# Operand and x transposes moved to DMA, and the hash to 32x32 VectorE transposes with row and column tiles, in a hash-bucketed attention kernel with a gated feed-forward part

## The chip, the cores and the metric

One core of one Trainium2 chip. The metric is the device time of one execution in microseconds (us), lower is better. Executions of one kernel were repeated; medians of them are given. A run is called slow when it is more than 1.5% above the fastest of the same kernel, else fast. A median over slow and fast runs is not comparable between kernels, so differences below are taken between the means of fast runs.

## The reference, cut to what matters

```python
def _attn_ref(q, k, v, proj):                 # q, k, v: (4, 8, 768, 64) float32; proj: (64, 6)
    q_bits = (einsum('bhsd,dk->bhsk', q, proj) > 0)      # 6 hash bits per token
    k_bits = (einsum('bhsd,dk->bhsk', k, proj) > 0)
    mask = q_bucket[:, :, :, None] == k_bucket[:, :, None, :]   # buckets from the bits
    scores = where(mask, q @ k^T / 8, -1e9)
    return softmax(scores) @ v
x = attn_out.transpose(0, 2, 1, 3).reshape(3072, 512)
def _moe_ref(x, w_gate, w_val, w_out, w_res): # 512 -> 1536 -> 512
    ffn_out = (gelu(x @ w_gate) * (x @ w_val)) @ w_out
    return x + sigmoid(x @ w_res) * ffn_out
```

The mask costs no instruction of its own. Each operand of a score matmul has 64 feature rows, 6 rows of bits (+-0.5) and one constant row, 71 in all. With q scaled by 1/C, C = 2048, a pair of different buckets loses at least half a unit in the score (one bit that differs turns +0.25 into -0.25), and the exponential, which multiplies by C/8 = 256, makes it zero.

## The kernel before

16 pairs of heads, two pairs to a group, so eight groups. A group is prepared in one piece while the group ahead of it runs: loads, fp32 transposes of q and k on TensorE, evacuation by VectorE, casts, hash, bit copies.

```python
def prep(g):
    for pi in range(2):                                   # two pairs
        for side, src in ((0, q), (1, k)):
            nc.sync.dma_start(s, ...)                     # 384 KB
            for (c0, n) in CH:                            # TensorE transposes, fp32 128x128
                for c in range(n):
                    nc.tensor.transpose(ps[:, bass.ts(c, P)], s[:, hi, bass.ts(tp, P)], ident)
                nc.vector.tensor_scalar_mul(tt[...], ps[...], (1.0 / C) if side == 0 else 1.0)
            nc.gpsimd.tensor_copy(ag[0:D, :, 0, :], t3[0:D])
            nc.vector.tensor_copy(ag[0:D, :, 1, :], t3[D:2 * D])
        ...                                               # v: load, casts, sum (unchanged)
    for (t0, n) in CH:                                    # hash: 128 rows, 32 columns per tile
        for pi in range(2):
            for side in range(2):
                nc.tensor.matmul(hs[32 * j:32 * j + 32, :n * P], projw, t32[pi, side][...], ...)
        nc.vector.tensor_scalar(bits[...], hs[...], 0.0, cst, op0=ALU.is_gt, op1=ALU.add)
    ...                                                   # 8 bit copies by DMA into aug[D:KA]

def attn(p):
    for c in range(0, len(bk), 2):                        # 9 steps per pair, 18 per group
        sp = sc_ps.tile([P, 1024], FP32, tag="sp")
        ...  nc.tensor.matmul(sp[...], ks[...], qs[...])  # scores: 71 rows, 1024 columns in all
        nc.scalar.activation(e, sp, AF.Exp, scale=float(ALPHA))
        ...  nc.tensor.matmul(av[hi][:, qt, :], e[...], va[...])   # 8 value products, 65 columns
```

Ahead of the value products of each head stands one more matmul, 128x128 on 390 columns, which starts their sum ("av<-vsum,eps_sb" in the timelines): four of these initial products to a group.

After attention comes a dense feed-forward part whose matmuls are all 128 x 128 x 512.

The softmax here doesn't subtract the row's maximum and nothing guards it: scores larger than these inputs give would overflow.

## Time and profile before

| kernel before | value | where from |
|---|---|---|
| median time | 421.25 us (418.3 to 421.97) | 3 runs |
| first score matmul | 30.9 us | timeline |
| attention, first score to last exponential's use | 31 to 209 us | sums over stretches |
| exponentials | 144, 1.02 us each | group lines |
| feed-forward | 211.7 us | timeline |
| TensorE busy in attention | 157.3 of 178 us | sums over stretches |

The lines behind these are in the prediction. Two more matter later, because the prediction did not look at them. They are TensorE groups kept apart by shape, kernel before; the columns are count, busy us, mean ns of one, idle time before them.

```profile
L212 PE MATMUL sp<-aug,aug 71*128 71x512 bf16 x192 | 66.2, 388 | 0.0
L137 PE MATMUL tp<-ident,ld 128*128 128x128 f32 x192 | 33.9, 314 | 7.6 <-DMA ld<-in_q_dram 3.9 <-DVE t L139 3.6
```

A score matmul of 512 columns takes 388 ns in the mean, in a kernel whose work between the scores includes 192 transposes that use the whole 128 x 128 array. "71\*128" is the part of the array that a matmul uses: 71 rows, 128 columns.

### The profile page before, as it was taken

How to read it: one execution, taken by the hardware profiler on the slowest of the kernel's cores; microseconds unless marked ns; L12 is line 12 of the kernel's file. 1: busy time of each engine (PE TensorE's matmuls, PEld its weight loads, DVE VectorE, ACT ScalarE, POOL GpSimd, SP SyncE). 2: the span in 40 equal slices, each digit the busy share in tenths (PEclk: the TensorE clock that was granted, in tenths of full speed). 3: DMA queues.
4: the chain of work that ended last, by engine and by line, in shares of the span. 5: the costliest groups of instructions: out<-in, count | busy, mean ns of one | idle time of the engine just before them, and what ended most of it. 6: DMA issues, size and time to landing. Idle time of an engine off the chain costs nothing.

```text
span 421.1 us, 7282 instructions
## 1 busy us (share of the span) xinstructions
PE 381.9 (91%) x2924; PEld 199.4 (47%) x2944; DVE 184.3 (44%) x315; ACT 200.2 (48%) x242; POOL 101.2 (24%) x157
## 2 busy tenths in 40 slices
PE   1788988879989898989799999999999999999995
PEld 1454555645565456545444444444444444444442
DVE  1674362936355274631234433344343334334433
ACT  1008879587977768789643123223213313312321
POOL 4961662835558362720000000000000000000000
PEclk9999999999999699999899999999999999999999
DMA  7802728348184732300000110010020010011001
GB/s 244 279 8 86 263 83 297 104 141 298 37 296 158 239 141 86 112 10 2 2 0 0 51 51 2 25 75 2 5 81 15 0 76 25 0 52 50 1 27 75
DMA packets 23138, 36.82 MB, mean 87 GB/s; under 512 B 4672, under 2 KB 16960, under 8 KB 23104
## 3 DMA queue, kind: packets, MB, share of 16 engines
q1 hardware_dynamic: 23104, 36.35, 24.9%
q8 instruction: 23, 0.38, 0.4%
q14 instruction: 11, 0.09, 0.1%
HBM read 29.36 MB, written 6.29 MB: 85 GB/s over the span
## 4 chain that ended last, share of the span: by engine, by line
PE 67%; ACT 10%; DVE 8%; DMA 5%; issue 4%; POOL 3%; SPq 2%; ACTq 0%; DVEq 0%; POOLq 0%
PE gps L276 15%; PE vps L282 15%; PE fps L294 15%; ACT e L217 10%; PE sp L212 6%; PE av L230 5%; PE rps L288 5%; DVE t L139 3%; DVE aug L145 3%; PE tp L137 3%; DMA wtmp<-in_moe_w_out_dram 2%; PE hs L166 2%; DMA ld<-in_k_dram 2%; DMA ld<-in_q_dram 1%; SPq L176 1%
## 5 line engine op out<-in xcount | busy, mean ns | idle before, releaser
L217 ACT ACTIVATE e<-sp 128x1024 bf16<-128x1024 f32 x144 | 140.4, 1021 | 63.6 <-PE sp L212 59.4
L212 PE MATMUL sp<-aug,aug 71*128 71x256 bf16 (+1 forms) x384 | 86.9, 332 | 0.0
L279 ACT ACTIVATE gt<-gps 128x512 bf16<-128x512 f32 x72 | 43.0, 597 | 88.5 <-PE gps L276 85.1
L284 DVE TENSOR_TENSOR hh<-gt,vps 128x512 bf16<-128x512 bf16 x72 | 49.5, 687 | 74.0 <-PE vps L282 67.0
L230 PE MATMUL av<-va,e 128*128 128x65 bf16 x1152 | 61.7, 196 | 14.5 <-ACT e L217 10.5
L276 PE MATMUL gps<-x_sb,wg 128*128 128x512 bf16 x282 | 73.9, 383 | 0.3
L282 PE MATMUL vps<-x_sb,wv 128*128 128x512 bf16 x283 | 73.2, 379 | 0.3
L230 PEld LDWEIGHTS <-e 128*128 128x128 bf16 x1152 | 46.3, 99 | 53.7 <-ACT e L217 49.0
L294 PE MATMUL fps<-wo,hh 128*128 128x512 bf16 x281 | 65.5, 379 | 0.4
L139 DVE TENSOR_SCALAR t<-tp 128x512 f32<-128x512 f32 x64 | 32.8, 550 | 28.1 <-PE tp L137 24.8
L276 PEld LDWEIGHTS <-wg 128*128 128x128 bf16 x288 | 28.4, 99 | 34.6 <-issue 1.1
L144 POOL CAST aug<-t 64x768 bf16<-64x768 f32 x32 | 33.9, 1063 | 45.1 <-DVE t L139 24.9
L282 PEld LDWEIGHTS <-wv 128*128 128x128 bf16 x288 | 28.2, 98 | 34.3 <-issue 0.5
L294 PEld LDWEIGHTS <-hh 128*128 128x128 bf16 x288 | 28.2, 98 | 34.0
L291 ACT ACTIVATE th<-rps 128x512 f32<-128x512 f32 x24 | 14.3, 597 | 61.7 <-PE rps L288 58.9
L137 PE MATMUL tp<-ident,ld 128*128 128x128 f32 x192 | 33.9, 314 | 7.6 <-DMA ld<-in_q_dram 3.9
L298 DVE SCALAR_TENSOR_TENSOR o<-th,fps 128x512 f32<-128x512 f32 x24 | 16.5, 687 | 52.4 <-PE fps L294 49.6
L212 PEld LDWEIGHTS <-aug 71*128 71x128 bf16 x384 | 29.3, 99 | 8.4 <-issue 1.0
L137 PEld LDWEIGHTS tp<-ident,ld 128*128 128x128 f32 x192 | 25.7, 161 | 14.0 <-DVE t L139 6.8
L201 DVE RECIPROCAL rec<-av 128x6 f32<-128x6 f32 x32 | 6.1, 192 | 54.9 <-PE av L230 54.9
L145 DVE CAST aug<-t 64x768 bf16<-64x768 f32 x32 | 28.9, 904 | 2.6 <-PE sp L212 1.7
L288 PE MATMUL rps<-wr,x_sb 128*128 128x512 bf16 x94 | 25.1, 387 | 0.3 <-issue 0.2
(34 smaller groups left out, 186.9 us busy)
## 6 DMA issues: line engine op xcount, KB each, us to landing
ld<-in_q_dram SPq DMA_DIRECT2D x16, 384.0 KB
ld<-in_k_dram SPq DMA_DIRECT2D x16, 384.0 KB
ldv<-in_v_dram SPq DMA_DIRECT2D x16, 384.0 KB
out_dram<-o SPq DMA_DIRECT2D x24, 256.0 KB
wtmp<-in_moe_w_gate_dram SPq DMA_DIRECT2D x4, 768.0 KB
wtmp<-in_moe_w_val_dram SPq DMA_DIRECT2D x4, 768.0 KB
wtmp<-in_moe_w_out_dram SPq DMA_DIRECT2D x4, 768.0 KB
aug<-bits SPq DMA_DIRECT2D x64, 10.5 KB
```

Source lines behind the costliest of these rows:

```text
L137: nc.tensor.transpose(ps[:, bass.ts(c, P)], s[:, hi, bass.ts(tp, P)], ident)
L139: nc.vector.tensor_scalar_mul(tt[:, c0 * P:(c0 + n) * P], ps[:, :n * P], (1.0 / C) if side == 0 else 1.0)
L145: nc.vector.tensor_copy(ag[0:D, :, 1, :], t3[D:2 * D])
L212: nc.tensor.matmul(sp[:, off:off + nq * P], ks[hi][:, bass.ts(jt, P)], qs[hi][:, qt0 * P:(qt0 + nq) * P], start=True, stop=True)
L217: nc.scalar.activation(e, sp, AF.Exp, scale=float(ALPHA))
L230: nc.tensor.matmul(av[hi][:, qt, :], e[:, off:off + P], va[:, hi, jt, 0:D + 1], start=False, stop=(jt == T - 1), skip_group_check=True)
L276: nc.tensor.matmul(gps, wg[:, kk, bass.ts(m, P)], xr[:, kk, :], start=(kk == 0), stop=(kk == KM - 1))
L279: nc.scalar.activation(gt, gps, AF.Gelu)
L282: nc.tensor.matmul(vps, wv[:, kk, bass.ts(m, P)], xr[:, kk, :], start=(kk == 0), stop=(kk == KM - 1))
L284: nc.vector.tensor_mul(hh[:, m, :], gt, vps)
L288: nc.tensor.matmul(rps, xr[:, kk, bass.ts(tt, P)], wr[:, kk, :], start=(kk == 0), stop=(kk == KM - 1))
L294: nc.tensor.matmul(fps, hh[:, m, bass.ts(tt, P)], wo[:, m, :], start=(m == 0), stop=(m == KF - 1))
```

## The change

Its intent is to take the transposes off TensorE and to let prep run in small pieces between the scores. Operands are cast to bf16 (zero padded from 64 to 128 columns) and transposed by DMA; x is transposed by DMA too; the hash takes 32x32 block transposes of the fp32 data from VectorE, and multiplies them in 32-row, 32-column tiles of the array, several at once; the conversion, hash and weight loads are handed out one piece per exponential; the value products lag one exponential behind. Cut to its core:

```diff
-                        for c in range(n):
-                            nc.tensor.transpose(ps[:, bass.ts(c, P)], s[:, hi, bass.ts(tp, P)], ident)
-                        nc.vector.tensor_scalar_mul(tt[...], ps[:, :n * P], ...)
+                n = nat[(2 * p + side) % NN]              # 128 x 12 x 128 bf16, half of it zeros
+                nc.gpsimd.tensor_copy(n[:, :, 0:D], s)
+                nc.sync.dma_start_transpose(out=ag, in_=n.rearrange("p c n -> p (c n)"))
+                nc.vector.transpose(tt..., s...)          # 32x32 blocks, fp32
...
-                        nc.tensor.matmul(hs[32 * j:32 * j + 32, :n * P], projw, t32[pi, side][...])
+            for a0 in (0, 2):
+                for c0, c1 in ((0, HT // 2), (HT // 2, HT)):
+                    for dh in range(2):
+                        for j, t in enumerate(src):       # four operands: column tile j
+                            for i in range(2):            # row tile a = a0 + i
+                                nc.tensor.matmul(hs[i][32 * j:32 * j + 32, c0:c1, :],
+                                    projw[32 * a:32 * a + 32, dh, :],
+                                    t[32 * a:32 * a + 32, c0:c1, dh, :],
+                                    start=(dh == 0), stop=(dh == 1),
+                                    tile_position=(32 * a, 32 * j))
+                    yield                                 # one piece of side work
...
         def xpose(b):
-            for kk in range(KM):  ... nc.tensor.transpose(...); nc.vector.tensor_copy(...)
+            for t in range(b * T, (b + 1) * T):
+                nc.sync.dma_start_transpose(out=x_sb[:, t], in_=x_tok[:, t, :])
...
+        def ahead(g):                                     # side work of group g, in pieces
+            convert(2g+2); yield; convert(2g+3); yield
+            load(2g+4); load(2g+5); three weight pieces (g >= 1); yield
+            yield from hashes((2g+2, 2g+3))               # ends with 4 bit copies by DMA
```

The score and value matmuls are unchanged in shape and number.

## The prediction

> **What bounds the kernel now.** I read the page first (engine shares, the 40 slices, the groups), then the sums over three stretches, then the timeline of a quiet piece and of the start, and last the chain in order of time where it stalls. The first group line gives the exponentials of the attention, the sums over stretches give the stages.

> ```profile
> span 421.1 us, 7282 instructions
> L217 ACT ACTIVATE e<-sp 128x1024 bf16<-128x1024 f32 x144 | 140.4, 1021 | 63.6 <-PE sp L212 59.4
> 0.00:31.00 31.00, 17.89 (x83) 10.77 (x84) 16.40 (x30) 1.28 (x1) 21.88 (x48) 1.00 0.55 180
> 31.00:208.00 177.00, 156.50 (x1903) 94.58 (x1902) 84.75 (x166) 140.36 (x144) 79.35 (x109) 0.98 0.41 140
> 208.00:421.10 213.10, 207.54 (x940) 94.07 (x958) 83.11 (x121) 58.59 (x97) 0.00 (x0) 0.99 0.08 30
> ```

> There are three stages. Up to 31 us nothing is exponentiated. From 31 to 208 us 144 exponentials run, 140.4 of 177 us. From 208 us on the feed-forward part keeps TensorE busy for 207.5 of 213.1 us. The change leaves that last stage's 960 matmuls as they are (only the strides of x differ), so what can be won lies in the first 208 us. A quiet piece shows the pace that attention could have:

> ```profile
> 185.80 5.08 ACT L217 ACTIVATE e<-sp 128x1024 bf16<-128x1024 f32 x5
> 187.79 0.42 PE L230 MATMUL av<-va,e 128*128 128x65 bf16 x8
> 188.05 0.60 PE L212 MATMUL sp<-aug,aug 71*128 71x256 bf16 x3
> 188.91 0.42 PE L230 MATMUL av<-va,e 128*128 128x65 bf16 x8 [0.26 <-ACT e L217]
> ```

> Five exponentials in 5.08 us are 1.016 us each. TensorE needs 188.05-187.79 = 0.26 us for eight value products and about 0.44 us for 1024 score columns (1024 in two such calls of 0.60 us, less a tail of about 0.17), so 0.70 us per exponential: 0.32 us of it is slack. A group of two pairs is 18 exponentials, 18.3 us at this pace; eight groups are 146 us. The stage takes 177, so 31 us are lost there, to prep work that holds TensorE's queue and to two DMA stalls, which the chain shows:

> ```profile
> 114.76 5.95 DMA ld<-in_q_dram
> 120.71 1.20 POOL aug L144
> 121.91 1.42 POOL wr L97
> 123.34 4.17 DMA wtmp<-in_moe_w_out_dram
> 131.45 4.92 DMA wtmp<-in_moe_w_out_dram
> 136.42 1.46 POOL wo L97
> 166.36 6.55 DMA ld<-in_k_dram
> ```

> The one in-order queue that issues DMAs (SyncE) waits for a staging buffer of weights, and the small copies of hash bits behind it come late. And the start is serial: transposes and hashes of four pairs come ahead of the first score (first transpose at 3.9, first score at 30.9 us in the views of these tiles).

> [...] The kernel before has no DMA transpose[...] it has the hash in four column tiles: 16 records in 1.50 us at 103.27 us, where 4 x 2 passes of 512 and 256 columns one after the other would be several times that, so the tiles do run beside one another.

> **The change, part by part.**

> *TensorE, removed.* 192 fp32 transposes (33.9 us busy), 96 transposes of x (9.9 us) and the 64 hash matmuls (14.0 us): 57.8 us busy. Per group about 4 x 0.8 + 1.5 + 1.2 = 5.9 us, of which the 0.32 us of slack per exponential hides perhaps half.

> *TensorE, added.* 64 hash matmuls per group, each 32x32x192 in fp32, two passes each. In the trace before a pass over 512 columns took 0.43 us (hash weight loads at 103.27, 103.72, 104.15 us), so 192 columns take 0.16 us. A piece of 16 is 32 pairs of load and matmul; eight tiles at once would need 4 x 0.16 = 0.65 us, but pairs start no closer than the value products, 0.26/8 = 0.033 us, so 32 x 0.033 = 1.05 us. Per group 4.2 us[...]. The built order shows that the scheduler does not leave these as evenly spread pieces: from the third group on about 50 of the 64 stand in one lump between two pairs' scores, where ScalarE starves. So I take 18.3 + 2.5 = 20.8 us per group with hashes, against about 21 before (18 exponentials at 1.15 us in its undisturbed stretches). Almost no gain here.

> *VectorE.* Off: evacuations 32.8, casts 28.9, x copies 8.9 us. On: 32 block transposes (768 fp32 columns, estimated 0.9 us each from 0.55 us per 512-column pass of before, so 29 us) and bit compares (64 of 384 columns at about 0.5 us, at most 32 us, was 9.2). It falls by some 20 us, and it is nowhere the bound in attention (84.8 of 177 us).

> *GpSimd.* 32 casts (33.9 us) become 30 casts of 128x768 (the same cast of v takes 0.89 us), about 28 us. Neutral.

> *Start.* Data of q arrive at 3.9 us. Now only pair 0 needs to be done for the first score: conversions on ScalarE, two DMA transposes, a hash of 32 matmuls, and the bit copies. The copies stand in the queue behind three or four loads of the next group[...]; at 244-279 GB/s (first slices) 384 KB take 1.5 us. I get: loads of pair 0 landed 7, [...]loads ahead of the bits issued by 16, bits landed 20, first score 21 us. Gain: 10 us.

> *SyncE and DMA.* This is the term that decides. Per group the queue carries 4 operand transposes of 384 KB (half of it zero padding), on average 3 transposes of x of 128 KB, 6 loads, in five groups 3 weight pieces of 768 KB, and 4 bit copies. [...] Issue per group: [...]6 x 0.45 + 3 x 0.4 + 4 x 0.78 (rows of this queue before) = 19.4 us, just under the 20.8. But the third weight piece waits for the first to land and be cast, and it stands ahead of three of the four bit copies: [...]loads of 2.3 MB at 300 GB/s 7.9, weight 2.6, cast 1.5, the rest of the issues 2.8: about 25 us. In those five groups I therefore allow 23 us, as part of it overlaps with what a group has in hand.

> *Sum.* Start 21; the first group 20.8; five groups with weights 5 x 23 = 115; two more, of which the last has no hash, 20.8 + 18.5 = 39.3; feed-forward 212.5 (the last x transposes are needed only by its round 4, so they hide): 408.6. As a scheme often overlaps a little better than a serial sum, I put 406 us, 3.6% under the 421.25.

> **The rivals.**

> *A: transposes cheap.* If a transpose costs 1.3 us or less[...], the queue has 7 us to spare per group, the stalls of 166 and 115 us disappear, and attention is bound by ScalarE with hash bubbles: 20 + 7 x 20 + 18.5 + 212.5 = 391 us. For it: loads are issued one group earlier than before. Against it: the weights still stand ahead of the bits.

> *B: the DMA queue becomes the bound.* If an operand transpose takes 5 us, a group needs 20 + 4 + 7 = 31 us, and attention 8 x 31: 21 + 248 + 212.5 = 481 us; with 3.5 us it is about 440. For it: the queue already produced the two stalls of before without any transpose. Against it: half the queue's time is idle before (mean 140 GB/s in attention).

> *C: the hash is the new wait.* If small tiles start only every 0.06 us, a group gets another 4 us, most of it in front of ScalarE: 8 x 4, about 430 us. The eight value products in 0.26 us speak against it.

> **Range and chances.** I give A 35%, the middle course 40%, B and C together 25%. A is nearly always under 412.8 us, the middle course is in a bit more than half its cases, B and C seldom: faster 0.59. The middle course's rest and mild forms of B fall within 2%: 0.19. Over 429.7 us: 0.22. Eight times in ten between 383 and 446 us.

> **What would show it.** Right: first score matmul near 21 us; TensorE without the transposes, hash busy time some 30 us in all; exponentials at 1.15-1.3 us apiece over attention, and ScalarE's idle time ended by scores that waited for a transpose or for bits in the middle groups; last stage 212-214 us; an operand transpose occupying SyncE's queue for 2-3 us. Wrong: that queue showing transposes of over 4 us (B) or under 1.5 us (A); hash matmuls with gaps above 0.05 us (C); the feed-forward stage longer than 215 us because strided x slows its matmuls, which I hold for unlikely.

Where a cut is marked, the passage told of DMA transposes, of the hash's tiles or of the queue what no trace of this case had shown. The issue of a group came to 19.4 us with two terms that are cut, those of the operand and the x transposes; the three that stand make 7.0. The 25 us of a group with weights had a cut term for four transposes; what stands makes 14.8. The times of the start had a step for the first two transposes, and the 4.2 us of the hash a term that is cut. The forecast's sum came to 408.6 us, put at 406, with these terms in it: its 21, 20.8 and 23 us rest in part on estimates that were not shown, and so do the 2-3 us of an operand transpose among the signs; the rivals' 1.3, 3.5 and 5 us are suppositions. Beside figures that stand: the two passes of an fp32 hash matmul are the 128 records of the 64 matmuls before (L166), the 300 GB/s are the 296 to 298 of its fullest slices, and a compare of 384 columns, put at about 0.5 us, took 605 ns in the changed kernel (mean of L190).

## The result, and the profile after

The changed kernel takes 509.44 us in the median of 4 runs (495.76 to 516.4); beside them the kernel before took 420.03. Two of the four are fast, with a mean of 499.1 us against 420.1. The ratio is 1.188, 95% interval 1.171 to 1.206. Here and below a ratio is the mean time of one kernel's fast runs over that of the other's fast runs of the same rounds, so it is not quite the ratio of the medians, and can differ a little from that of the means in the table. The profiled run was one of the slow ones (516.4 us); the fast ones, 495.76 and 502.52, are still 18 and 20% over the kernel before, and the profiles of e2, e3 and e4 below, all of fast runs, show the same thing as this one.

First the page and the groups of the changed kernel, against the lines of before.

```profile
span 514.6 us, 8440 instructions
PEclk9999999999999999555555569999999999999998
L251 ACT ACTIVATE e<-sp 128x1024 bf16<-128x1024 f32 x144 | 146.3, 1024 | 148.0 <-PE sp L246 147.7
L246 PE MATMUL sp<-aug,aug 71*128 71x512 bf16 x192 | 107.0, 608 | 4.6 <-DMA aug<-bits 4.6
L181 PE MATMUL hs<-t,projw 32*32 32x192 f32 x1024 | 84.1, 498 | 12.9 <-DVE bits L190 6.4 <-DVE t L152 6.4
```

The exponential still takes 1.02 us, but ScalarE now waits 147.7 us for scores (59.4 before). TensorE itself waits little: 4.6 us for bits ahead of the scores, 12.9 ahead of the hash. The same 512-column score matmul takes 608 ns instead of 388. So it is not that TensorE waits for the new transposes; it is slower at work that nobody changed.

The sums over three stretches (start, attention, feed-forward) place it. The columns are us, then busy us and count for PE, PEld, DVE, ACT and POOL, the granted clock, DMA share, GB/s.

```profile
0.00:24.40 24.40, 14.36 (x130) 8.29 (x130) 9.80 (x15) 2.97 (x3) 14.78 (x38) 1.00 0.92 247
24.40:300.60 276.20, 266.09 (x2463) 132.17 (x2462) 63.63 (x118) 146.26 (x144) 75.40 (x115) 0.83 0.57 142
300.60:514.60 214.00, 208.33 (x953) 94.30 (x962) 83.41 (x122) 58.61 (x97) 0.00 (x0) 0.99 0.10 34
220.00:240.00 20.00, 20.00 (x142) 9.69 (x141) 5.14 (x9) 12.41 (x13) 9.28 (x14) 0.50 0.48 166
```

The pace can be read without the clock record, from the start times. The end of attention in the changed kernel (timeline, scores and value products):

```profile
295.37 1.04 PE L246 MATMUL sp<-aug,aug 71*128 71x512 bf16 x2
296.29 0.62 PE L231 MATMUL av<-va,e 128*128 128x65 bf16 x8
296.72 1.04 PE L246 MATMUL sp<-aug,aug 71*128 71x256 bf16 x3
297.59 0.62 PE L231 MATMUL av<-va,e 128*128 128x65 bf16 x8
...
300.67 1.90 PE L318 MATMUL gps<-x_sb,wg 128*128 128x512 bf16 x4
302.36 1.73 PE L324 MATMUL vps<-x_sb,wv 128*128 128x512 bf16 x4
303.92 1.03 PE L318 MATMUL gps<-x_sb,wg 128*128 128x512 bf16 x4
```

From one group of scores to the next, 296.72 - 295.37 = 1.35 us pass, from scores to value products 0.87 to 0.92 and from these to the next scores 0.43, where the quiet piece of before had 0.44 for the scores and 0.26 for eight value products. So the scores run at half the pace, and the value products at some 0.6 of it. And they do until the dense feed-forward matmuls have run for some 3 us: the first four take 1.69 us until the next begin, and from about 304 us on four take the 0.86 us that the rest of the stage shows.

I counted, in every run, the recorded score matmuls of 512 columns that took more than 500 ns (half pace; the expectations call these matmuls half-tile scores) and in which stretches they lie. Before: 7 of 192, between 139 and 145 us. After: 179 of 192, from 24 to 190 and from 211 to 298 us. The clock record is not a safe guide to this: it shows 9 for the slices up to some 206 us of the changed kernel, where the durations say half, and in all of e8 below (mean 0.998) it stays near full speed, while 160 of 192 of these matmuls run at half pace. So I go by durations.

How the pace goes and comes back can be seen in the kernel before, in its only spell at half pace (timeline):

```profile
137.36 0.60 PE L212 MATMUL sp<-aug,aug 71*128 71x256 bf16 x3
139.03 0.33 PE L223 MATMUL av<-vsum,eps_sb 128*128 128x390 bf16 x1 [1.07 <-POOL aug L144]
139.20 0.45 PE L230 MATMUL av<-va,e 128*128 128x65 bf16 x8
139.46 1.04 PE L212 MATMUL sp<-aug,aug 71*128 71x512 bf16 x3
...
145.02 1.04 PE L212 MATMUL sp<-aug,aug 71*128 71x512 bf16 x2
145.86 0.59 PE L230 MATMUL av<-va,e 128*128 128x65 bf16 x8
146.29 0.60 PE L212 MATMUL sp<-aug,aug 71*128 71x256 bf16 x3
```

After a wait of 1.07 us a group of scores takes 1.04 instead of 0.60 us, and 7 us later 0.60 again. No transpose runs on TensorE in these 7 us, only scores, value products and one initial product, so the state can end without other work. In the changed kernel the same state lasts for 166 us. The question for the experiments is what ends it so late.

### The profile page after: what moved, and what is told of

The parts are those of the page before. It is cut to its first block, busy times and chain, and to the rows that moved or that the text cites. A ratio compares the mean times of both kernels' runs of the same rounds, so it can differ in the third digit from the quotient of the medians.

```text
span 514.6 us, 8440 instructions
## 1 busy us (share of the span) xinstructions
PE 488.8 (95%) x3540; PEld 234.8 (46%) x3552; DVE 156.8 (30%) x255; ACT 207.8 (40%) x244; POOL 90.2 (18%) x152
## 4 chain that ended last, share of the span: by engine, by line
PE 88%; DMA 4%; SPq 2%; ACT 1%; POOL 1%; DVE 1%; issue 1%; DVEq 0%; ACTq 0%; POOLq 0%
PE sp L246 21%; PE hs L181 13%; PE gps L318 12%; PE vps L324 12%; PE fps L336 12%; PE av L231 12%; PE rps L330 4%; SPq L149 2%; DMA ld<-in_q_dram 2%; PE av L224 1%; ACT e L251 1%; DMA aug<-bits 1%; DMA ldv<-in_v_dram 1%; DMA ld<-in_k_dram 1%; DVE bits L190 1%
## 5 line engine op out<-in xcount | busy, mean ns | idle before, releaser
L251 ACT ACTIVATE e<-sp 128x1024 bf16<-128x1024 f32 x144 | 146.3, 1024 | 148.0 <-PE sp L246 147.7
L246 PE MATMUL sp<-aug,aug 71*128 71x256 bf16 (+1 forms) x384 | 144.6, 507 | 4.6 <-DMA aug<-bits 4.6
L231 PEld LDWEIGHTS <-e 128*128 128x128 bf16 x1152 | 73.2, 128 | 72.0 <-issue 35.9
L181 PE MATMUL hs<-t,projw 32*32 32x192 f32 x1024 | 84.1, 498 | 12.9 <-DVE bits L190 6.4
L231 PE MATMUL av<-va,e 128*128 128x65 bf16 x1152 | 88.5, 241 | 2.7 <-ACT e L251 2.3
L181 PEld LDWEIGHTS hs<-t,projw 32*32 32x32 f32 x1024 | 32.3, 143 | 51.0 <-issue 19.4
L246 PEld LDWEIGHTS <-aug 71*128 71x128 bf16 x384 | 40.5, 134 | 31.6 <-issue 23.4
L152 DVE STREAM_TRANSPOSE t<-ld 128x768 f32<-128x768 f32 x32 | 30.4, 965 | 26.1 <-DMA ld<-in_q_dram 15.4
L190 DVE TENSOR_SCALAR bits<-hs,cst 128x384 bf16<-128x384 f32 (+1 forms) x36 | 20.3, 605 | 34.6 <-PE hs L181 34.6
L157 POOL CAST va<-ldv 128x768 bf16<-128x768 f32 x16 | 13.2, 827 | 59.2 <-PE av L231 50.1
```

Of the source, the lines that this page charges most:

```text
L152: nc.vector.transpose(tt.rearrange("p c h n -> p (c h n)"), s.rearrange("p c d -> p (c d)"))
L181: nc.tensor.matmul(hs[i][32 * j:32 * j + 32, c0:c1, :], projw[32 * a:32 * a + 32, dh, :], t[32 * a:32 * a + 32, c0:c1, dh, :], start=(dh = ...
L190: nc.vector.tensor_scalar(bits[:n, :, 32 * a:32 * a + 32], hs[i][:n], 0.0, cst[:n], op0=ALU.is_gt, op1=ALU.add)
L231: nc.tensor.matmul(av[hi][:, qt, :], e[:, off:off + P], va[:, hi, jt, 0:D + 1], start=False, stop=(jt == T - 1), skip_group_check=True)
L246: nc.tensor.matmul(sp[:, off:off + nq * P], ks[0:KA, hi * T + jt, :], qs[0:KA, hi * T + qt0:hi * T + qt0 + nq, :], start=True, stop=True)
```

## The experiments

Four theories. **Rows**: with 71 of 128 rows in the scores and 32x32 tiles in the hash, too little of the array works for the half pace to end. **Two states**: a full pace, once reached, holds itself until a wait. **Tiles**: the 32x32 hash tiles hold the pace down. **Queue**: the in-order DMA queue is what costs time; the pace is a by-product of its stalls. (In order: in the changed kernel the queue issues nothing from 196.8 to 205.3 us, then one weight piece, and at 205.71 the three bit copies behind it, though the first copy of the same bits was issued at 196.01.) The stretch of 220 to 240 us above, 20.00 of 20.00 us busy at half pace, says that busy time alone is not what counts.

All edits below are to the changed kernel. Their results, with the kernel before on the same chip and in the same rounds (medians 421.7 to 423.4 us; 420.03 for the first line); "half pace" is the count defined above, of the 512-column scores that the trace recorded (192 in every kernel; where fewer are given, records are missing). The count is of one profile each, and that was a slow run for after, e1, e6, e8, e9, e13 and e17:

| run | edit | median us, all runs | mean us, fast runs | ratio to before (95%) | half pace |
|---|---|---|---|---|---|
| (after) | none | 509.44 | 499.1 (of 2) | 1.188 (1.171 to 1.206) | 179 of 192 |
| e1_k128 | scores of 128 rows | 452.3 | 450.8 | 1.070 (1.062 to 1.079) | 43 of 192 |
| e2_kick | 20 dense matmuls before the first score | 488.39 | 482.9 (of 2) | 1.146 (1.134 to 1.158) | 80 of 192 |
| e3_no_hash | no hash matmuls (wrong result) | 472.24 | 470.5 | 1.125 (1.115 to 1.134) | 144 of 192 |
| e4_x_on_pe | x transposes on TensorE | 507.42 | 507.9 | 1.205 (1.200 to 1.211) | 130 of 192 |
| e5_k128_late | e1, weights after the bits | 438.95 | 438.6 | 1.039 (1.034 to 1.045) | 11 of 157 |
| e6_k128_late_xpe | e5 and e4 | 426.81 | 423.6 (of 2) | 1.003 (0.993 to 1.013) | 9 of 155 |
| e7_kick_late_xpe | e2, weights late, e4 | 438.87 | 438.2 | 1.038 (1.033 to 1.043) | 23 of 192 |
| e8_late | weights late alone | 516.55 | 498.4 (of 1) | none (one fast run) | 160 of 192 |
| e9_k96_late_xpe | e6 with 96 rows | 449.2 | 443.8 (of 2) | 1.054 (1.039 to 1.069) | 55 of 192 |
| e10_dense_hash_71 | dense hash, weights late, e4 | 420.38 | 420.4 | 0.998 (0.990 to 1.006) | 9 of 192 |
| e11_half_transposes | e6 without padding, weights spread | 424.65 | 423.4 | 1.005 (0.993 to 1.017) | 10 of 154 |
| e12_dense_hash_half | e11 with dense hash | 431.01 | 431.5 | 1.022 (1.012 to 1.032) | 2 of 164 |
| e13_dense_hash_only | dense hash alone | 435.52 | 428.1 (of 2) | 1.013 (1.004 to 1.022) | 48 of 192 |
| e14_split_71 | e10, fewer compares | 427.3 | 426.6 | 1.009 (1.002 to 1.016) | 15 of 192 |
| e15_split_128 | e14, 128 rows, weights spread | 420.06 | 420.0 | 0.993 (0.986 to 1.001) | 4 of 165 |
| e16_split_half | e14, half transposes, weights spread | 419.59 | 420.5 | 1.007 (0.987 to 1.027) | 13 of 192 |
| e17_dense_filler | useless dense matmuls added | 437.84 | 437.6 | 1.035 (1.027 to 1.043) | 16 of 192 |

All but e3_no_hash gave the reference's result.

### One suspect at a time (e1 to e4)

**e1_k128.** Rows 71 to 127 of both operands are zeros from the padding, so they can be contracted without changing a result.

```diff
-  nc.tensor.matmul(sp[...], ks[0:KA, hi * T + jt, :], qs[0:KA, hi * T + qt0:..., :], ...)
+  nc.tensor.matmul(sp[...], ks[0:P, hi * T + jt, :],  qs[0:P, hi * T + qt0:..., :], ...)
```

> Edit: the score matmuls contract all 128 rows (rows 71 to 127 of both operands are zeros) in place of 71; the result and the column count are the same. Theory 1 (TensorE ran attention at half pace because its clock is released by how much of the array works, and 71 rows with 32x32 hash tiles are too little): 1024 score columns take about 0.43 us instead of 0.85 over most of attention, total 395 to 430 us. Theory 2 (the clock needs one dense stretch to be released, then holds), theory 3 (the small hash tiles hold it down) and theory 4 (the DMA queue is the bound): nothing changes, 495 to 516 us.

452.3 us: the same matmuls, more rows of zeros, 48 us less (fast runs). The page of that run has the mean of all score matmuls at 367 ns, where the changed kernel has 507 and the kernel before 332:

```profile
L246 PE MATMUL sp<-aug,aug 128*128 128x256 bf16 (+1 forms) x384 | 98.4, 367 | 5.9 <-DMA aug<-bits 5.9
```

The half pace lasts until 43 us, and later only 3 to 8 us after each of four waits (9.0, 1.3, 3.4, 4.4 us long, at 89.7, 138.5, 154.4 and 169.9 us) and after two lumps of hash pieces that no long wait precedes (109 to 113 us, and from 197 us, where more pieces follow until 207 us). So with nothing but the rows changed the half pace ends sooner here (43 of 192 scores against 179), and these two times it came on after a lump of 32x32 tiles.

**e2_kick.** Twenty dense bf16 matmuls of 512 columns between the first hashes and the first score.

```diff
+        for i in range(20):
+            nc.tensor.matmul(wk[:, 512 * (i % 2):...], aug[0, 1][:, 0, :], aug[0, 0][:, 0:4, :], start=True, stop=True)
```

> Edit: 20 dense matmuls of 128x128x512 (bf16, into a score buffer nobody reads) right before the first score. Theory 2: full pace from there on, at least up to the first long wait of TensorE, 400 to 440 us in all. Theory 1 and 3: full pace for a few us, then half pace again, 495 to 520 us. Theory 4: 495 to 525 us whatever the pace.

488.39 us, between the expected ranges. From 29 to 88 us the scores of 71 rows run at full pace, 64 of them in a row; then come two waits (2.9 us at 88.5, 3.4 us at 92.2), and the half pace is back for 68 us. The clock of this profile shows the same shape:

```profile
span 478.3 us, 8493 instructions
PEclk9999999755555595555599999999999999999999
```

So there are two states, each of which lasts for tens of us under the same work. Both losses of the full pace in this profile follow waits of TensorE of 2.9 to 4.0 us.

**e3_no_hash.** All hash matmuls out, bits zero (a wrong result).

> Edit: no hash matmuls at all; the bit rows are zeros made by VectorE from the block transposes, so the result is wrong on purpose (no mask), while every DMA and every score stays. Theory 3: full pace, 385 to 415 us. Theory 1: half pace stays, 144 x 1.3 us of TensorE plus start and feed-forward, 420 to 445 us. Theory 4: above 470 us, as the DMA queue is untouched.

472.24 us: 29 us less than the changed kernel (fast runs), as a whole kind of work is gone. By its time alone the run falls to the queue theory (above 470); but TensorE now waits 34 us for VectorE, which is busy for 110 us of attention here against 64 in the changed kernel, as it makes the bit rows; so the pace decides, not the time. 144 of 192 scores are still at half pace. In this stretch there is no hash and no idle time (sums over a stretch):

```profile
144.00:164.00 20.00, 20.00 (x160) 10.67 (x158) 4.62 (x10) 14.66 (x15) 1.98 (x3) 0.50 0.90 185
```

With scores of 71 rows, value products and the initial products alone, four spells at half pace last about 10 to 74 us each (15.9 to 89, 113 to 123, 137 to 196, 204 to 235 us); each does end. The tiles are not needed for the loss.

**e4_x_on_pe.** The x transposes back to TensorE and VectorE, as before.

> Edit: only the transposes of x go back to TensorE and VectorE as in the kernel before; operands and hash stay as changed. Theory 4: the 20 us stall near 190 us, where the in-order DMA queue held operand transposes and loads behind x transposes, goes away: 475 to 490 us. Theories 1 to 3: 490 to 516 us, TensorE still at half pace in attention, since 96 bf16 transposes are little.

507.42 us. In attention no wait of TensorE over 1 us is left; the stall of the changed kernel near 206 us (4.6 us, for the bits behind the x transposes) is gone, and the time is no shorter (507.9 against 499.1 us, fast runs). The trace shows one thing more: three of its four spells at half pace end while a batch's x transposes, dense 128x128 matmuls, run on TensorE (these begin at 79.2, 152.0 and 227.6 us, and the last slow scores begin at 81.7, 153.1 and 228.7).

### Both together (e5 to e9)

The weights' pieces stand ahead of the bit copies in the queue. "Late" moves them behind:

```diff
-            if g >= 1:
-                for _ in range(3): wload.pop(0)()
             yield
             if g + 1 < NG:
                 yield from hashes((2 * g + 2, 2 * g + 3))
+            if g >= 1:
+                for _ in range(3): wload.pop(0)()
```

Expected of e5_k128_late:

> Scores contract all 128 rows as in e1_k128, and the weight pieces are issued after the copies of the hash bits instead of ahead of them. e1_k128 (452 us) still lost time in four waits in attention (9.0, 1.3, 3.4 and 4.4 us) and in the half-pace spells after each. If the weights ahead of the bits cause those waits, they go and with them the spells: start 24, eight groups at 20 to 21, feed-forward 213, about 400 to 410 us. If the x transposes, which hold the queue, cause them, it stays at 440 to 452.

Expected of e6_k128_late_xpe:

> e5_k128_late with the transposes of x back on TensorE and VectorE, so that nothing in the DMA queue waits for the end of a batch's attention. If both the row count and the queue matter, this is the fastest so far: about 395 to 410 us, no wait over 1 us in attention, under 20 of 192 half-tile scores at half pace. If full rows alone are not enough to keep TensorE's pace through group boundaries and lumps of hash pieces, 425 or more.

Expected of e7_kick_late_xpe:

> Scores contract 71 rows as the change has it; twenty dense matmuls before the first score; weights after the bits and x transposes on TensorE, so no stall of the queue. If the pace once released lasts as long as no wait interrupts, this is within 10 us of e6_k128_late_xpe plus 5 us for the dense matmuls (400 to 420). If 71 rows lose the pace at group boundaries even without stalls, it falls to half pace for 40 to 70 us each time: 450 to 490 us.

Expected of e8_late:

> The changed kernel with only the weight pieces moved behind the bit copies: 71 rows, no dense matmuls, x transposes by DMA. The theory that the DMA queue costs the time expects the stalls near 115 and 206 us to go and 430 to 460 us. The theory of the half pace expects that the stall only hid work that TensorE had to do anyway: 490 to 510 us, with over 150 of 192 half-tile scores still at half pace.

e8_late alone changes nothing for the better (its one fast run 498.4 us against 499.1), although no wait of TensorE over 0.7 us is left in its attention: the queue theory falls. With full rows the same edit is worth 12 us (450.8 to 438.6, fast runs), and x on TensorE another 15 (to 423.6). e5 missed its 400 to 410, and e6 its 395 to 410. e7 missed too, at 438.87 instead of 400 to 420: the full pace of 71-row scores, once reached, lasted from 30 to 134 us (with x transposes on TensorE in between), and was lost after a wait of 2.6 us at 131; it came back only 36 us later, when the next x transposes started on TensorE (171.0 us).

e6, e4 and e9 form a series in the number of rows, x on TensorE in all three (the weights late in e6 and e9):

> e6_k128_late_xpe (427 us, 9 half-tile scores at half pace) with scores that contract 96 rows instead of 128; 71 rows without dense matmuls gave 507 us in e4_x_on_pe. The added rows hold zeros, so no result changes. If the share of the array's rows at work decides how soon the pace is released, this lies between: 430 to 480 us, with a half-pace part of the first 20 to 50 us. If 71 rows were slow for another reason (an odd count, a tile shape), 96 behaves as 128 does: within 8 us of 427.

71 rows: 507.9 us in fast runs, 130 at half pace; 96 rows: 443.8 (all runs 442 to 470), 55; 128 rows: 423.6, 9. It is graded, so not an oddity of the number 71. (The 71-row run lacks the late weights; e8 showed that at 71 rows these gain nothing.) The spread of the 96-row runs fits a case near the edge, but no run shows a threshold.

### The hash instead of the scores (e10, e13, e17)

A dense hash: the projection is laid block-diagonally over the four 32-row blocks, and two matmuls of 128 rows, 128 columns and 384 moved columns do one operand. The compares go straight into the operand's bit rows, so there are no bit copies.

```diff
-  projw[32 * a:32 * a + 32, :, 0:NBITS]              # 32 columns, sixteen 32x32 matmuls per operand
+  projw[32 * a:32 * a + 32, :, 32 * a:32 * a + NBITS]   # 128 columns
+  for dh in range(2):
+      nc.tensor.matmul(hs, projw[:, dh, :], t[:, :, dh, :], start=(dh == 0), stop=(dh == 1))
+  for r in range(4):
+      nc.vector.tensor_scalar(ag[D:KA, :, 32*r:32*r+32], hs[32*r:32*r+NROW], 0.0, csts[side][...], is_gt, add)
```

> Scores contract 71 rows, no extra dense matmuls at the start, weights after the bits, x transposes on TensorE; but the hash is two 128-row, 128-column matmuls per operand (the projection block-diagonal over the four 32-row blocks) instead of sixteen 32x32 ones, and VectorE compares straight into the operand. Same 32x32 block transposes. This gives TensorE back dense work like that of the kernel before, some 8 matmuls of 384 fp32 columns per group. If it is dense work here and there that keeps the pace in the kernel before, most of attention now runs at full pace: 400 to 440 us. If 71-row scores lose it whatever the hash is, 480 to 500 us.

420.38 us with 71-row scores and 9 of 192 at half pace. This run also moved the weights and x; e13 undoes the hash alone.

> The changed kernel with one part undone: the hash is two 128-row, 128-column matmuls per operand again dense on the array, with the compares on VectorE straight into the operand (so no bit copies in the queue). Scores of 71 rows, operand and x transposes by DMA, weights where the change has them. If the loss comes from the hash having no dense work, nearly all of it comes back: 415 to 435 us, most half-tile scores at full pace. If moving the weights and x (which e10_dense_hash_71 also did) was needed as well, 440 to 490.

435.52 us in the median of two fast runs (427.73 and 428.51, inside the expected 415 to 435) and two slow ones (442.53 and 442.58), at the edge of it. Between fast runs, one part undone gives back 71 of the 79 us between the two kernels (499.1 to 428.1, and 420.1 before); the edits to the queue (e10 against e13) give some 8 more. The profile is of a slow run. In e13 the pace is lost after four waits of 1.8 to 9.5 us and is back 4 to 7 us after each, as long as there are hashes to do. The last of them ends at 181.9 us. At 186 us a short wait takes the pace away, and now it does not come back: the 37 half-tile scores left all run at half pace. Whether the fast runs have this last spell is not known, as none was profiled. The timeline shows the loss:

```profile
184.91 0.60 PE L236 MATMUL sp<-aug,aug 71*128 71x256 bf16 x3
186.29 0.33 PE L214 MATMUL av<-vsum,eps_sb 128*128 128x390 bf16 x1 [0.78 <-DVE x_tok L204]
186.87 1.04 PE L236 MATMUL sp<-aug,aug 71*128 71x512 bf16 x3
```

The groups of that run:

```profile
L236 PE MATMUL sp<-aug,aug 71*128 71x256 bf16 (+1 forms) x384 | 102.2, 375 | 0.2 <-ACT e L241 0.2
L179 PE MATMUL hs<-t,projw 128*128 128x384 f32 x128 | 58.5, 557 | 19.3 <-DVE aug L182 11.2
```

This leaves two readings: dense matmuls supply something, or small tiles take something away. (e13 also took the bit copies out of the queue; e17 leaves them there.) e17 keeps the tiles and adds useless work.

```diff
                 hs = [hs_ps.tile([P, HT, 32], FP32, tag="hs", name="hs") for _ in range(2)]
+                for i in range(2):
+                    for _ in range(6):
+                        nc.tensor.matmul(hs[i], eps_sb, eps_sb.unsqueeze(1).to_broadcast([P, 3, P]), start=True, stop=True)
```

> The changed kernel with its 32x32 hash tiles kept, and in front of each quarter of them twelve useless dense bf16 matmuls (128x128, 384 columns) into the same accumulators, which the hash then overwrites: 24 a group, 0.16 us each at full pace, about 3.9 us a group, so 31 us of added work. If it is the lack of dense work that leaves TensorE at half pace, the added work makes the kernel faster: 440 to 475 us, with far fewer than 179 of 192 half-tile scores at half pace. If the 32x32 tiles themselves hold the pace down, it gets slower by 31 to 60 us: 535 to 570.

(The 0.16 us is an estimate, from the 0.86 us above of four matmuls of 512 columns.)

437.84 us, even a little under the 440 to 475 of the first reading: more work, 62 us less (fast runs). (By the code the twelve stand in front of each half of a hash, not of each quarter; 24 a group is right.) The groups (page of that run):

```profile
L251 PE MATMUL sp<-aug,aug 71*128 71x256 bf16 (+1 forms) x384 | 91.3, 341 | 14.2 <-DMA aug<-bits 7.6
L178 PE MATMUL hs<-eps_sb 128*128 128x384 bf16 x216 | 56.3, 366 | 5.8 <-DVE bits L195 3.8
L186 PE MATMUL hs<-t,projw 32*32 32x192 f32 x1024 | 32.7, 341 | 1.0 <-DVE t L152 1.0
```

The mean score falls to 341 ns, near the 332 of the kernel before, with the 32x32 tiles in place. (The two hash lines overlap in time; their busy times are not to be compared.) So dense work here and there is what the changed kernel lacks: e13 and e17 put it back in two ways, and e1 reaches the same by filling the rows. What is not shown is how long a spell lasts: with scores, value products and initial products alone it ended after 7 us in the kernel before and after 10 to 74 us in e3. Nor did any run take dense matmuls out of the kernel before.

### Why the cured kernels only equal the kernel before (e11, e12, e14 to e16)

With the pace back, the DMA engines are full. The first 121 us of attention in e6 and, second, of the kernel before (sums over a stretch; the last three columns are clock, DMA share, GB/s):

```profile
24.00:145.00 121.00, 109.88 (x1715) 62.13 (x1738) 49.38 (x91) 91.08 (x93) 61.17 (x96) 0.99 0.98 239
```

```profile
24.00:145.00 121.00, 106.75 (x1248) 64.17 (x1247) 62.77 (x118) 90.31 (x93) 63.72 (x86) 0.98 0.49 167
```

A share of 0.98 against 0.49. The page's queue line gives the cost of one operand transpose:

```profile
q1 hardware_dynamic: 70432, 48.93, 45.5%
```

```profile
q1 hardware_dynamic: 23104, 36.35, 24.9%
```

For e6 (first) 45.5% of 425.2 us is 193.5 us of all 16 engines; before (second) 24.9% of 421.1 is 104.9. The difference of 88.6 us over the 32 operand transposes that e6 has more is about 2.8 us each. That is an upper estimate, as other packets were a little slower too: the 256-byte packets of e6's trace, which are these transposes, add up to 81.1 us of all 16 engines, 2.5 each.

e11 halves those bytes: two heads' columns in one 128-column tile, VectorE copies the halves into place; weights two pieces per group. e12 adds the dense hash to it. e14 takes e10's 128 small compares (79 us on VectorE) apart into 32 whole ones and small copies; e15 adds 128 rows; e16 has e14 with unpadded transposes written straight into every other column block.

Expected of e11_half_transposes:

> e6_k128_late_xpe had the 16 DMA engines busy all through attention (share 1.00 from 24 to 180 us), so at full pace the DMA is the next bound. Here the operand transposes carry no zero padding (two heads' columns share a 128x128 tile; VectorE copies both halves into the operand), which halves their bytes, and weights come two pieces per group instead of three. 128-row scores, x on TensorE. If DMA engines bound e6, this gains 10 to 20 us: 405 to 415. If the hash pieces on TensorE bound it, it stays at 420 to 428.

Expected of e12_dense_hash_half:

> e11_half_transposes with the dense hash of e10_dense_hash_71: half the transposes' bytes, 128-row scores, weights two per group, no copies of bits in the queue. With neither DMA nor small hash tiles in the way, attention should be bound by the exponentials: 18.5 to 19.5 us per group, first score near 20 us: 385 to 400 us, faster than both kernels. Over 410 if the sixteen small compares per group on VectorE (about 0.5 us each) hold the hash up.

Expected of e14_split_71:

> e10_dense_hash_71 (420 us) had 128 compares of 7 rows at 615 ns on VectorE, 79 us, and they stand in the chain with 11%. Here one compare of 128 rows per operand writes a tile of bits, and four small copies, two on GpSimd and two on VectorE, place them. If those compares hold the hash and so the start of each group up, 405 to 415 us; if not, 418 to 423.

Expected of e15_split_128:

> e14_split_71 with scores that contract 128 rows and two weight pieces per group instead of three. Against e14 it tells whether, with dense hashes, full rows still add anything: half-pace spells of e10 covered 9 of 192 half-tile scores, so at most 3 us from the pace; the spread of the weights may give a few more where the DMA engines are full. 400 to 415 us; if DMA engines are the bound, equal to e14.

Expected of e16_split_half:

> e15_split_128 (420 us, profile 415) had the DMA engines full from 24 to 145 us (share about 1.0) and waits for operand transposes of 5.8, 8.3 and 6.7 us in its chain. Here the transposes carry no zero padding: 768 columns instead of 1536 per operand, written into the even columns of the operand; VectorE moves the other head's half into the odd columns. Scores contract 71 rows, the hash is dense, weights two per group, x on TensorE. If the padding's DMA time is what holds the cured kernel, 395 to 410 us, faster than both kernels; if VectorE's longer chain (32 copies of about 0.5 us more) takes its place, 412 to 425.

e11 was 424.65 us and e16 419.59, each in the second branch of its expectation: the DMA work fell (the queue's share from 45.5% to 37.6% and 35.1%), the time hardly. So full DMA engines are not alone the bound. e12 missed widely (431.01 instead of 385 to 400): VectorE is busy 35 of 36 us from 24 to 60 us there, and TensorE waits 14.8 us in all for its compares (615 ns each). e14 missed (427.3, in neither branch and above e10), and e15 missed its range by 5 us (420.06). In e16 the chain of waits from 20 to 56 us is almost all VectorE's small copies (those of the other head's half took 625 ns each), compares and transposes. Here each cure of one engine loaded another (VectorE is busy 157 us in the changed kernel, 261 in e12, 214 in e16). No version beat the kernel before beyond the noise: e15, the fastest by ratio, is 0.993, interval 0.986 to 1.001. What holds the cured kernel at 420 is therefore not settled as one cause; a balance of DMA, VectorE and hash work is what these runs suggest, without showing it.

## Why the prediction was wrong

It said 406 us, range 383 to 446; the kernel took 509. By its own steps:

- **"TensorE needs ... 0.70 us per exponential: 0.32 us of it is slack."** This is the step that failed. It was read off a quiet piece of before and carried over as a property of the work. After the change TensorE needed 0.85 + 0.44 = 1.29 us, more than the exponential's 1.02, so TensorE became the bound. (The reading has one slip: 1024 columns are one line of 0.60 us, not two; the 0.44 is right.) The premise under it, that taking dense matmuls off TensorE only makes it emptier, is what e13 and e17 refute: put dense matmuls back, and most of attention runs at full pace again. Of the 79 us between fast runs, 71 come back with a dense hash alone. No rival had this in it, and none of the signs that the prediction named was the duration of a score matmul.
- **"The first group 20.8; five groups ... 23."** A group took (300.6 - 24.4) / 8 = 34.5 us. Summed from the start of each TensorE record to the start of the next, from 24.4 to 300.6 us of the trace, and divided by eight: scores and value products 23.6 us (18 x 1.31), hash 8.2, initial products 1.4, idle 1.3, in all 34.5. So the error is mainly one factor, the pace, in nearly every term; the stalls are small.
- **"A piece of 16 is ... 1.05 us. Per group 4.2 us."** The piece is right at full pace: 32 records took 1.17 and 1.18 us in e6's chain, and 1.46 us at half pace. The group is too low: by the same sum the hash took 5.8 us of TensorE for each of the seven groups in e6, and 9.4 in the changed kernel. The scheduler cuts it into smaller pieces, and these are dear: two records at 107.76 us of e1 took 0.44 us until the next start, fourteen at 108.55 took 0.48. Rival C had such a cost, but not as a matter of pace; with no hash at all (e3) the kernel still takes 470.5 us, so C is not the cause.
- **"SyncE and DMA. This is the term that decides."** It did not decide: e4 and e8 took its stalls away for nothing. An operand transpose held SyncE's queue for 1.74 us in the median here, not the 2 to 3 named as a sign, and an x transpose, with a third of the bytes, for 1.27 (changed kernel; the ns are min/median/max); in e6, with the DMA engines full, it was 2.53 (one in e13, at 38.85 us: 2.52):

```profile
L149 SPq DMA_TRANSPOSE aug<-nat x32: 1307/1742/4078, 5.2 to 256.4; - x32
L260 SPq DMA_TRANSPOSE x_sb<-x_tok x24: 1211/1266/2387, 102.2 to 308.2; - x24
```

One transpose took 2.5 to 2.8 us of all 16 engines (e6). The sum of the issue cost has a slip as well, in a cut term: three x transposes carry 3 x 128 KB, as much as one operand, and were counted as three quarters of one. At full pace the queue is worth 12 + 15 us (e1, e5, e6), and some 8 from e13 to e10: Rival B in a mild form is there, behind the pace.
- **"First score 21 us"**: 24.4. **"Feed-forward 212.5"**: 214.0, some 1.5 us of it the first matmuls still at half pace. Both small.
- **Would the plan have paid at full pace?** As far as these runs tell, no: e1, the plan with only the rows filled and most scores at full pace, takes 450.8 us, and e10, with a full pace, another hash and an eased queue, starts at 19.2 us, ends at 211.8 us of feed-forward, and needs 187.6 us between, where the prediction's groups add up to 175.1. It equals the kernel before.

## What to carry to other kernels

Before taking matmuls off TensorE, ask what keeps the array at full pace, and compare the duration of an untouched matmul before and after: if it grew much (0.60 to 1.04 us for 1024 score columns here), look for the pace first and for waits second. If most of what is left contracts few rows or uses small tiles, try filling the operands up to 128 rows (zeros do; 48 us less in e1) or a dense form of a small product in place of many tiles, even where it does more arithmetic (71 us less in e13). And here a stall was worth removing only when its engine was not the bound in a slower state: the same edit gained nothing at half pace (e8) and 12 us at mostly full pace (e1 to e5).
